# Second layer of tile 0 first and once for all kinds of steps, the third tile in a branch behind it, and evictions as one ScalarE operation

## The chip, the core and the metric

The program runs on one core of one Trainium2 chip. Times are device microseconds (us) of one launch, from the first to the last instruction of the core and the little that lies around it. The core has five engines with a queue each: TensorE (PE; its weight loads are listed apart as PEld), VectorE (DVE), ScalarE (ACT), GpSimd (POOL) and SyncE (SP). Each engine has a sequencer that reads its instructions, takes the branches and loads registers itself, and hands the rest to the engine; in the rows its instructions carry a q (PEldq, ACTq).

## The reference

Linear attention with positive random features on 8 batches of 8 heads, and then a mixture of 8 experts in which each of the 4608 tokens goes to one expert:

```python
    q_p, k_p = (phi(q_s), phi(k_s))
    kv = np.einsum('bhsm,bhsd->bhmd', k_p, v)
    ...
    return (num / den).astype(np.float32)
...
    expert_idx = np.argmax(logits, axis=1)
    ...
    for e in range(E):
        mask = expert_idx == e
        xe = x[mask]
        h = np.maximum(xe @ w1[e], 0.0)
        ye = h @ w2[e]
        out[mask] = gate_w[mask, None] * ye
```

x has 512 columns, the hidden layer 1024. The change lies in the experts alone, in `h @ w2[e]` and the scaling by the gate.

## The kernel before

The first part of the program (attention, and the routing that sorts tokens by expert) is written out without branches. Its result lies in DRAM as rows of tokens, which the second part gathers by index.

The second part runs in steps, one after the other, each for one expert. A step has two tiles of 128 tokens (256 columns in the first layer), and at the end of an expert perhaps a third one, full or of up to 64 tokens. So there are three kinds of steps, known only at run time: a register `kind` holds 2 for a step of two tiles, 1 for one with a half third tile ("short"), 0 for one with a full third tile. Every step is written out once, with all its variants, and branches on all engines pick one. `step` (L1134) issues, in this order: transposing loads for the next step; a split of new weights, where the expert changes; the first layer `l1`, in two parts with three variants each; gathers for a later step; `following()`, which prepares the input of the next step on ACT and DVE; and the second layer (L1149 to L1158).

Matrices are split into a high and a low part (`hh`, `hl`; `w2h`, `w2l`, both "w2p" in the rows), and three products are added. `l2(t, a)` (L1068) is the second layer of one tile: 24 matmuls of 512 columns, 3 for each of 8 chunks of the hidden layer. Its sum lies in a PSUM bank of its own: p_t for tile 0, p_snu for tile 1, p_skv for the third tile. `l2half` (L1081) does the short tile in 16 matmuls and needs a chain of ACT, DVE and ACT to evict. `send` (L1100) evicts a bank in halves, one by ACT (L1102) and one by DVE (L1103), both scaled by the gate, and `scatter` (L1106) writes the rows to the output by index on POOL, one scatter after the other.

The order on each engine is that of the code. Before, a step of kind 2 runs l2 of tile 0, loads a flag into a register (`reg`, L961) and runs l2 of tile 1 inside `when` (L1111). A step of another kind jumps behind that (L1149), runs the third tile (short or full, L1153) and then tiles 0 and 1 without asking. So the second layer of tiles 0 and 1 stands in the program twice.

What the code doesn't show is how an If is closed. Semaphores count the finished instructions of an engine, and all ways through an If must leave the same count. Where a way issues fewer instructions than another, the missing count is added to one of its own instructions; a way that issues nothing on an engine gets an instruction of the sequencer, which waits until the engine's own count stands where it should and then adds the rest. In the listings of the order it shows as a branch that "waits" for its own engine.

Of the kernel before, what the change touches and what calls it, by code (L numbers as in the profile page):

```python
# [14 lines left out]
AF = mybir.ActivationFunctionType  # L15
# [6 lines left out]
DM = H * D  # L22
# [824 lines left out]
class Experts:  # L847
# [121 lines left out]
    def split(self, n, cs=range(8)):  # L969
        for c in cs:  # L970
            split_r(self.nc, *self.part(n, c), self.nc.scalar, self.nc.vector)
# [126 lines left out]
        self.send(p, self.ys[i % 3], self.gt[i % 6], idx[:, i:i + 1])  # L1098

    def send(self, p, y, gate, idx):  # L1100
        c = DM // 2
        self.nc.scalar.activation(y[:, :c], p[:, :c], AF.Copy, scale=gate)  # L1102
        self.nc.vector.tensor_scalar_mul(y[:, c:], p[:, c:], gate)  # L1103
        self.scatter(y, idx)

    def scatter(self, y, idx):  # L1106
# [27 lines left out]
    def step(self, t, following, split=lambda: None):  # L1134
        engines = (ET.PE, ET.DVE, ET.Activation, ET.Pool)
        if t + 1 < NPR:
            self.flips(t + 1)
            self.flips3(t + 1)
        split()
        kind = self.kind(t, engines)  # L1140
        self.l1(t, kind)
        if t + 2 < NPR:
            self.gather(t + 2)
            self.gather3(t + 2)
        if t == 1:
            self.next(0, 2)
        following()
        self.nc.gpsimd.drain()
        with self.tc.If(kind > 1) as pair:  # L1149
            self.l2(t, 0)  # L1150
            self.when(self.reg(4, t, 1, engines), lambda: self.l2(t, 1))
        with pair.Else():
            with self.tc.If(kind > 0) as short:  # L1153
                self.l2half(t)
            with short.Else():
                self.l2(t, 2)
            for a in range(2):
                self.l2(t, a)  # L1158

    def tail(self, t):  # L1160
        split = lambda: self.change(t, 2)
# [103 lines left out]
```

## Time and profile before

| | us |
|---|---|
| median of 3 runs | 672.81 (671.24 to 673.86) |
| profiled execution, its own time | 671.42 |
| its span, first to last instruction | 669.4 |
| PE busy in the span | 639.6 (96%) |
| ACT, DVE, POOL busy | 409.7, 354.0, 280.1 |
| granted TensorE clock, mean | 0.997 |

The steps begin at about 270 us, the last matmul ends at 661.9 us. Busy time is that of engine instructions; register loads, branches and semaphore instructions aren't counted in it and are read line by line. Idle time is given with what ended it.

### The profile page before, as it was taken

To read this page: it belongs to the slowest core of one execution; us is meant where nothing else is said; L and a number is where in the kernel's file an instruction comes from. 1 tells how busy PE (TensorE), PEld (TensorE's weight loads), DVE (VectorE), ACT (ScalarE), POOL (GpSimd) and SP (SyncE) were. 2 spreads that over 40 slices of the span, in tenths; PEclk is the share of its full clock that TensorE was granted. 3 is DMA by queue.
4 is the path that set the end of the run, shared out by engine and by line. 5 is a ranking of instruction groups with operands and counts; after the bars stand their busy time and mean duration, and the time that the engine had idled before them with its cause. 6 is when DMAs were issued, how large, how long until landed. Compare 5 with 4: busy or idle time off the path is not lost. (4 is left out here: it accounts for less than half of the span.)

```text
span 669.4 us, 19369 instructions
## 1 busy us (share of the span) xinstructions
PE 639.6 (96%) x7185; PEld 579.0 (86%) x7185; DVE 354.0 (53%) x855; ACT 409.7 (61%) x1010; POOL 280.1 (42%) x499
## 2 busy tenths in 40 slices
PE   6898999999998989999999999999999999999995
PEld 5798999899898976788998989988989979989884
DVE  3467989989889978822222255222245255222220
ACT  6999999999999977633424166134256265243320
POOL 8576766676667932533330303312203303322111
PEclk9999999999999999999999999999999999999998
DMA  8864475655736342575641209543229509632101
GB/s 214 229 202 147 141 215 150 175 165 161 218 108 195 110 156 47 164 243 135 132 98 25 74 12 309 141 91 76 66 67 257 155 12 273 186 87 49 41 12 39
DMA packets 113247, 90.01 MB, mean 134 GB/s; under 512 B 72126, under 2 KB 96702, under 8 KB 113088
## 3 DMA queue, kind: packets, MB, share of 16 engines
q1 hardware_dynamic: 105360, 68.78, 38.6%
q0 software_dynamic: 7184, 19.04, 8.5%
q8 instruction: 92, 1.51, 0.9%
q14 instruction: 67, 0.55, 0.3%
q10 hardware_dynamic: 544, 0.13, 0.1%
HBM read 63.46 MB, written 19.15 MB: 123 GB/s over the span
## 5 line engine op out<-in xcount | busy, mean ns | idle before, releaser
L1032 PE MATMUL p<-xh,w1p 128*128 128x256 f32 (+2 forms) x960 | 148.0, 296 | 0.1
L1032 PEld LDWEIGHTS p<-xh,w1p 128*128 128x128 f32 x960 | 135.1, 188 | 2.5 <-issue 1.1
L1046 ACT ACTIVATE hh<-p 128x512 fp32r<-128x512 f32 (+2 forms) x84 | 43.6, 522 | 130.0 <-PE p L1032 126.1
L1047 DVE SCALAR_TENSOR_TENSOR hl<-p,hh 128x512 fp32r<-128x512 f32 (+2 forms) x84 | 48.1, 576 | 120.2 <-ACT hh L1046 117.3
L1107 POOL DMA_INDIRECT out_dram<-ys,idx x32 | 36.0, 1126 | 164.8 <-DVE ys L1103 57.6
L221 DVE TENSOR_REDUCE mx<-pp 128x8 f32<-128x1024 f32 x64 | 77.9, 1217 | 16.7 <-PE pp L214 16.3
L233 ACT ACTIVATE qp<-pp,mx 128x128 f32<-128x128 f32 x256 | 86.5, 585 | 0.0
L233 ACT ACTIVATE kp<-pp,mx 128x128 f32<-128x128 f32 x256 | 84.4, 547 | 2.7 <-DVE mx L221 2.0
L1032 PE MATMUL p<-xl,w1p 128*128 128x256 f32 (+2 forms) x480 | 83.3, 295 | 0.0
L214 PE MATMUL pp<-om_t,tq 64*128 64x128 f32 x1024 | 74.3, 284 | 3.9 <-ACT qp L233 3.0
L192 ACT COPY tq<-tt 128x1024 f32<-128x1024 f32 x59 | 73.3, 1243 | 0.9 <-PE tt L150 0.9
L1032 PEld LDWEIGHTS p<-xl,w1p 128*128 128x128 f32 x480 | 70.4, 188 | 0.0
L249 POOL TENSOR_TENSOR k<-kp 128x256 f32<-128x256 f32 x64 | 46.7, 730 | 52.6 <-ACT kp L233 49.0
L214 PEld LDWEIGHTS pp<-om_t,tq 64*128 64x128 f32 x1024 | 62.1, 187 | 7.5 <-ACT qp L233 4.5
L1006 ACT COPY xw<-xt 128x1024 uint16<-128x1024 uint16 x36 | 48.6, 1350 | 5.3 <-DMA xt<-xg 4.1
L1107 POOL DMA_INDIRECT out_dram<-y,idx x6 | 5.9, 986 | 105.6 <-DVE y L1103 56.5
L48 DVE TENSOR_TENSOR xl<-xw,xh 128x512 fp32r<-128x512 f32 x36 | 24.9, 693 | 46.6 <-ACT xh L54 36.8
L1102 ACT ACTIVATE ys<-p_snu,gt 128x256 f32<-128x256 f32 x16 | 7.6, 475 | 66.2 <-PE p_snu L1075 51.1
L1075 PE MATMUL p_t<-w2p,hl 128*128 128x512 f32 x120 | 47.0, 392 | 0.0
L1075 PE MATMUL p_snu<-w2p,hl 128*128 128x512 f32 x120 | 47.0, 391 | 0.0
L1073 PE MATMUL p_snu<-w2p,hh 128*128 128x512 f32 x120 | 47.0, 391 | 0.0
L1074 PE MATMUL p_t<-w2p,hh 128*128 128x512 f32 x120 | 47.0, 391 | 0.0
(407 smaller groups left out, 1337.3 us busy)
## 6 DMA issues: line engine op xcount, KB each, us to landing
w1s<-in_moe_w_dram SPq DMA_DIRECT2D x5, 2048.0 KB, 9.4
w2s<-in_moe_w_dram SPq DMA_DIRECT2D x5, 2048.0 KB, 10.5
v<-in_v_dram SPq DMA_DIRECT2D x32, 256.0 KB, 3.9
token_rows<-xc SPq DMA_DIRECT2D x8, 1024.0 KB, 4.8
k<-in_k_dram SPq DMA_DIRECT2D x31, 256.0 KB, 5.1
q<-in_q_dram SPq DMA_DIRECT2D x31, 256.0 KB, 5.5
kr<-in_k_dram SPq DMA_DIRECT2D x16, 64.0 KB, 3.6
vz<-in_v_dram SPq DMA_DIRECT2D x16, 64.0 KB, 3.9
```

Of the source, the lines that this page charges most:

```text
L192: self.nc.scalar.copy(self.pack(i, j), tt)
L214: nc.tensor.matmul(pp[:, a, n, i, :], th[r, k].rearrange("p a t -> p (a t)"), self.om[r, :], start=True, stop=True)
L221: nc.vector.tensor_reduce(out=mx[:, :, n], in_=s[("pp", h)][:, :, n], axis=AX.X, op=ALU.max, negate=True)
L233: nc.scalar.activation(x[:, j, :], pp[:, j % 2, n, j // 2, :], AF.Exp, bias=mx[:, j % 2, n, j // 2:j // 2 + 1])
L249: add = lambda o, x, y: nc.gpsimd.tensor_tensor(out=o, in0=x, in1=y, op=ALU.add)
L1006: self.nc.scalar.copy(x.bitcast(U16).rearrange("p c (t k) -> p k c t", k=2), xt.rearrange("p (k c) t -> p k c t", k=2))
L1032: self.nc.tensor.matmul(o, w[:, i, c], x[:, i, :], start=k == 0, stop=k == len(ops) - 1)
L1046: self.nc.scalar.activation(a[:, :, :n], o[:, :, :n], AF.Relu)
L1047: low = lambda d, c: self.nc.vector.scalar_tensor_tensor(out=d, in0=o[:, :, c], scalar=0.0, in1=a[:, :, c].bitcast(F32), op0=ALU.max, op1= ...
L1073: nc.tensor.matmul(p, h, self.w2h[:, c, :], start=c == 0, stop=False)
L1074: nc.tensor.matmul(p, h, self.w2l[:, c, :], start=False, stop=False)
L1075: nc.tensor.matmul(p, l, self.w2h[:, c, :], start=False, stop=c == self.NF - 1)
```

## The change

Every step now begins its second layer with tile 0, whatever its kind. Behind it stands an If without an Else for the third tile (`kind < 2`), and behind that tile 1, inside `when`, for all kinds. And `send` evicts a whole bank by one ACT instruction.

```diff
     def send(self, p, y, gate, idx):
-        c = DM // 2
-        self.nc.scalar.activation(y[:, :c], p[:, :c], AF.Copy, scale=gate)
-        self.nc.vector.tensor_scalar_mul(y[:, c:], p[:, c:], gate)
+        self.nc.scalar.activation(y, p, AF.Copy, scale=gate)
         self.scatter(y, idx)
...
-        with self.tc.If(kind > 1) as pair:
-            self.l2(t, 0)
-            self.when(self.reg(4, t, 1, engines), lambda: self.l2(t, 1))
-        with pair.Else():
+        self.l2(t, 0)
+        with self.tc.If(kind < 2):
             with self.tc.If(kind > 0) as short:
                 self.l2half(t)
             with short.Else():
                 self.l2(t, 2)
-            for a in range(2):
-                self.l2(t, a)
+        self.when(self.reg(4, t, 1, engines), lambda: self.l2(t, 1))
```

On PE, in the second layer of the first written-out step, this stood before between the matmuls of tile 0 (p_t) and tile 1 (p_snu) of a step of kind 2, and behind them (L1112 is `when`, L1153 the choice of the third tile; "ISA x2" are register operations):

```order
L1075 MATMUL p_t_5896<-w2p_5980,hl 128x512
L961 TENSOR_LOAD flags [waits DVE_49]
L961 ISA x2
L1112 COMPARE_AND_BRANCH
L1073 MATMUL p_snu<-w2p_5980,hh 128x512
...
L1112 UNCONDITIONAL_BRANCH
L1112 UNCONDITIONAL_BRANCH [waits PE_49]
L1153 COMPARE_AND_BRANCH
L1088 MATMUL p_skv<-w2p_5980,hh 128x512
```

The row that waits for PE itself is there the way on which tile 1 is left out. At the same place of PE this stands now (L1148 is the new If, L1149 the choice of the third tile, L1110 `when`):

```order
L1148 COMPARE_AND_BRANCH
L1149 COMPARE_AND_BRANCH
L1088 MATMUL p_skv<-w2p_5980,hh 128x512
...
L1149 UNCONDITIONAL_BRANCH
L1148 UNCONDITIONAL_BRANCH [waits PE_49]
L961 TENSOR_LOAD flags [waits DVE_49]
L961 ISA x2
L1110 COMPARE_AND_BRANCH
L1073 MATMUL p_snu<-w2p_5980,hh 128x512
```

The third tile has moved between the two tiles. The row that waits for PE itself is now the way of a step of kind 2, which has no third tile, and the register load and the branch stand behind it.

On ACT, in the same step, the difference of the evictions is this (ys and y are the rows to be scattered):

```order
-L1102 ACTIVATE ys_5989<-p_t_5896,gt 128x256
-L961 TENSOR_LOAD flags
-L1112 COMPARE_AND_BRANCH
-L1102 ACTIVATE ys_5987<-p_snu,gt 128x256
...
+L1101 ACTIVATE ys_5989<-p_t_5896,gt 128x512
+L1017 UNCONDITIONAL_BRANCH
+L1148 COMPARE_AND_BRANCH
+L1149 COMPARE_AND_BRANCH
+L1092 COPY y_5993<-p_skv 64x512
+L1094 ACTIVATE y_5993<-y_5993,gt 64x512
```

The evictions have twice the columns, tile 0's stands ahead of the third tile's, and the rows of DVE (L1103) are gone.

## Rows read from the trace of the kernel before

**Rows 1.** Busy time and granted clock by stretch (steps; the end).
```profile
core 0: us, PE busy (x) PEld busy (x) DVE busy (x) ACT busy (x) POOL busy (x), PEclk, DMA share, GB/s
335.00:663.00 328.00, 325.17 (x1873) 292.55 (x1871) 107.38 (x204) 131.28 (x211) 74.83 (x101) 1.00 0.39 105
663.00:669.40 6.40, 0.00 (x0) 0.00 (x0) 0.01 (x1) 0.00 (x0) 0.97 (x1) 0.67 0.14 51
```

**Rows 2.** Groups by line: busy us, mean ns | idle before, releaser.
```profile
L1075 PE MATMUL p_t<-w2p,hl 128*128 128x512 f32 x120 | 47.0, 392 | 0.0
L1075 PE MATMUL p_snu<-w2p,hl 128*128 128x512 f32 x120 | 47.0, 391 | 0.0
L1088 PE MATMUL p_skv<-w2p,hh 128*128 128x512 f32 x24 | 9.5, 396 | 1.6 <-DVE hh L1047 1.6
L1075 PE MATMUL p_skv<-w2p,hl 128*128 128x512 f32 x24 | 9.4, 393 | 0.0
```

**Rows 3.** Timeline of PE, 538 to 541: start, us, instruction [idle before].
```profile
538.03 0.75 PE L1032 MATMUL p<-xl,w1p 128*128 128x320 f32 x4
540.38 0.48 PE L1088 MATMUL p_skv<-w2p,hh 128*128 128x512 f32 x1 [1.60 <-DVE hh L1047]
```

**Rows 4.** Line 1149, then 1153, around 538: ns min/median/max, first to last start.
```profile
L1149 PEldq COMPARE_BRANCH  x1: 3141/3141/3141, 537.0 to 537.0; - x1
...
L1153 PEldq COMPARE_BRANCH  x1: 65/65/65, 540.1 to 540.1; - x1
```

**Rows 5.** Timeline of PE where tile 1 follows tile 0 (419).
```profile
419.25 0.39 PE L1075 MATMUL p_t<-w2p,hl 128*128 128x512 f32 x1
419.49 0.39 PE L1073 MATMUL p_snu<-w2p,hh 128*128 128x512 f32 x1
```

**Rows 6.** Line 1112 on PE's sequencer, 415 to 417.
```profile
L1112 PEldq COMPARE_BRANCH  x1: 65/65/65, 416.3 to 416.3; - x1
```

**Rows 7.** Timeline, the end: the last matmul, its eviction, the last scatter.
```profile
661.47 0.39 PE L1075 MATMUL p_snu<-w2p,hl 128*128 128x512 f32 x1
662.02 0.47 ACT L1102 ACTIVATE ys<-p_snu,gt 128x256 f32<-128x256 f32 x1 [5.15 <-PEq L1167]
662.53 0.48 DVE L1103 TENSOR_SCALAR ys<-p_snu,gt 128x256 f32<-128x256 f32 x1 [5.14 <-ACT ys L1102]
663.29 0.97 POOL L1107 DMA_INDIRECT out_dram<-ys,idx  x1 [4.62 <-POOLq L1149]
```

**Rows 8.** Line 1167 on PE's sequencer, 650 to 669.
```profile
L1167 PEldq COMPARE_BRANCH  x2: 181/1828/3474, 657.7 to 662.2; - x2
L1167 PEldq EVENT_SEMAPHORE  x2: 51/51/51, 661.9 to 662.0; - x2
```

**Rows 9.** Lines 1149, 961 and 1060 on PE's sequencer, 398.5 to 400.3.
```profile
L1149 PEldq EVENT_SEMAPHORE  x1: 51/51/51, 399.0 to 399.0; - x1
L961 PEldq TENSOR_LOAD <-flags x1: 307/307/307, 399.2 to 399.2; - x1
L961 PEldq FUSED_REGOPS  x1: 146/146/146, 399.6 to 399.6; - x1
L961 PEldq SEQ_ASSERT  x1: 18/18/18, 399.8 to 399.8; - x1
L1060 PEldq COMPARE_BRANCH  x1: 78/78/78, 399.9 to 399.9; - x1
```

**Rows 10.** Lines 961, 1060 and 1063 on PE's sequencer, all steps.
```profile
L961 PEldq TENSOR_LOAD <-flags x27: 297/308/656, 269.8 to 629.1; - x27
L1060 PEldq COMPARE_BRANCH  x48: 70/222/1893, 270.7 to 637.9; - x48
L1063 PEldq COMPARE_BRANCH  x18: 65/216/2711, 337.8 to 644.8; - x18
```

**Rows 11.** ACT instructions by line (1102, 930, 1094).
```profile
L1102 ACT ACTIVATE ys<-p_snu,gt x16: 474/475/477, 268.1 to 662.0; 128x256 f32<-128x256 f32 x16
L930 ACT ACTIVATE h<-p x4: 574/586/602, 257.2 to 258.7; 128x512 f32<-128x512 f32 x4
L1094 ACT ACTIVATE y<-y,gt x3: 724/724/724, 400.2 to 652.3; 64x512 f32<-64x512 f32 x3
```

## The prediction

> **What bounds the kernel now.** I read first the busy time by stretch [rows 1]: from 335 to 663 us, twelve of the steps, PE is busy for 325.17 of 328.00 us at the full granted clock, ACT for 131, DVE for 107, POOL for 75. The reader is to see that 2.83 us are left idle in all, so PE alone sets the time, an engine beside it costs nothing while PE isn't waiting for it, and anything that stops PE's queue is paid in full. Then where these 2.83 us lie. In the groups by line only one row of the second layer has idle time before it, the short third tile with 1.6 us [rows 2]; the timeline shows it once, at 540.38 [rows 3]. The rest is the end: the last matmul runs from 661.47 for 0.39 [rows 7], so it ends at 661.86, 1.14 us before 663.00. Third, the instructions of PE's sequencer, which aren't in busy time [rows 4, 6, 8 to 10].
>
> The counts of the groups also give the kinds of steps. p_t has 120 low products, 8 a step: 15 steps. p_skv has 24 of L1088, 8 a step: 3 short steps; and 24 of L1075: 3 with a full third tile [rows 2]. That leaves 15 - 3 - 3 = 9 steps of kind 2. All 15 have a tile 1 (p_snu x120).
>
> **The change part by part.** No matmul is added or removed. What changes is what stands between them.
>
> *The stall at 538 goes.* The profile puts it down to DVE, but that is the wait that came last in time; the branch row tells more. At 537.0 the jump over the two-tile variant took PE's sequencer 3.141 us, till 540.14, and only then the short tile's branch (540.1) and its first matmul (540.38) follow [rows 3, 4]. The last first-layer matmul began at about 538.5, so the jump began 1.5 us of queued work ahead and was not covered. In the changed program tile 0 follows the first layer without this jump, and the jumps of a third tile begin behind tile 0, whose matmuls are longer, 0.23 apart [rows 5]. At the one place where a branch among them can be timed, `when` at 416.3, the first matmul behind it began at 419.49: 3.2 us ahead [rows 5, 6]. That covers a jump of 3.141. Gain: the 1.60 idle and 0.09, by which the first matmul behind it is longer (0.48 against 0.39) [rows 3, 5]: 1.7 us. If the cover fails the gain is zero.
>
> *A wait is added in the nine steps of kind 2.* They have no third tile, so on the way round the new If PE's sequencer waits for PE's own count, behind the last matmul of tile 0, and adds the rest. Before, such a step only loaded a register there, 3.2 us ahead of need. Queued behind the wait are the register load, its operations, the branch, and all of tile 1. Does such a wait hold until the matmul has finished? The kernel before does it on PE once, at its end: the jump of 3.474 from 657.7 ends at 661.2, yet the semaphore instruction of the same line stands at 661.9, just behind the end of the last matmul at 661.86 [rows 7, 8]. It held the sequencer for 0.7 us, until nothing was left in PE. The Trainium skill (PSUM — Partial Sum Buffer, Engine vs sequencer instructions) says that the sequencer waits only for earlier instructions to be dispatched and not for their end; by that rule alone the bare addition would cost nothing and the sum would be rival A's. The row at 661.9 shows that the instruction here has a wait of its own.
>
> The price of one, from one matmul's start to the next, against the usual 0.23:
> - the last matmul of tile 0 runs 0.39 [rows 5]: 0.16 more;
> - from its end to the semaphore instruction, 661.86 to 661.9 [rows 7, 8]: 0.04;
> - semaphore instruction, register load, register operations, assertion, branch: the same five in the same order at the end of a step of another kind, from 399.0 to 399.9 + 0.08 [rows 9]: 0.95 (starts are given to a tenth);
> - from a branch's end to the first matmul of an empty PE, 540.1 + 0.065 to 540.38, with a semaphore instruction between [rows 3, 4]: 0.2, of which I take 0.12;
> - that first matmul, slower by 0.09 as above.
>
> 0.16 + 0.04 + 0.95 + 0.12 + 0.09 = 1.36 us, nine times: 12.2 us. Nothing covers it, since PE is what everything else waits for. From below: a wait alone, with the load somehow out of the way, would be 0.16 + 0.04 + 0.12 + 0.09 = 0.4, or 3.7 us in all; less than nothing is excluded, as the sequencer reaches the place 3.2 us early. From above: the slowest register load was 0.656, 0.35 over its median [rows 10], and the way round the If is itself a taken jump, of which the slowest on a similar place took 2.711 [rows 10], and the slowest of all 3.474 [rows 8]; 0.3 of that would be beyond a cover of 3.2: 2.0 each, 18 us. I take 1.36, since every piece is a row of its own, and the median load.
>
> *Steps of kinds 0 and 1.* They pass no such wait: both ways of the inner If have matmuls of their own to carry the count. The register load that they newly do (0.3 to 0.66 [rows 10]) lies 3 us ahead of need. Tile 0 needs the last chunk of the hidden layer only with its eighth chunk, 21 matmuls of 0.23 = 4.8 us in. Price zero; if PE did wait there, the only such wait of before, 1.6 [rows 3], is the bound.
>
> *Evictions.* Each goes from 0.475 on ACT and then 0.48 on DVE [rows 7, 11] to one ACT operation of 512 columns. No row shows one with a gate from PSUM: the nearest are 0.586 (512 columns from PSUM, no gate) and 0.724 (512 columns with the gate, from SBUF) [rows 11]; I take 0.70, nearer to that with the gate. Off the end it hides under PE: ACT is idle for more than half of the stretch, and no matmul waits for these banks until the next step's second layer, some 10 us on. At the end it is on the path: ACT 662.02, DVE until 663.01, scatter at 663.29 [rows 7]. Now the scatter may start at 662.02 + 0.70 + 0.28 = 663.00: 0.29 earlier; between 0.17 and 0.41 by the two rows. The last step has a short third tile, whose ACT, DVE, ACT chain now lies under tile 1's 24 matmuls (5.5 us). Should its scatter be late, the last one waits, and the 0.3 is lost.
>
> *Sum.* On the profiled execution's own time of 671.42 (span 669.4): + 12.2 - 1.7 - 0.3 = + 10.2, so 681.6. The median of the three runs, 672.81, lies 1.4 above it; I don't know which the new runs will be nearer to and add half: 682.3.
>
> **Rivals.**
> A, *the wait costs nothing* (the way round the If holds no wait in the chip's program, or PE has enough queued to bridge it). For it: PE has bridged nearly all branches until now. Against: a wait for one's own last matmul can't be bridged by one's own queue, and the row at 661.9. Then only the gains stay: 671.42 - 2.0 = 669.4, or 670.8 against the median. It is the way to "not slower", and decides once one wait costs less than 2.0 / 9 = 0.22 us.
> B, *the jump itself stalls*. The new If moves nine steps across a jump in the middle of the second layer. Jumps of PE mostly took 0.07 to 0.22, and a few took 1.893, 2.711, 3.141 and 3.474 [rows 4, 8, 10], at some places of the program and not at others. If all nine were slow ones, at 3.474 against a cover of 3.2, 0.3 each is added to the drain: 9 x 0.3 = 2.7, 685.0; if the cover were only the 1.5 of the place at 537.0, 2.0 each, 18, 700. Against: of 48 jumps of L1060 the median is 0.22 [rows 10]. The Trainium skill (Runtime: NRT & Kernel Launch, Instruction fetch mechanics) says that a taken branch whose target isn't in the fetched window must wait for a transfer of instructions; by it some of the nine would be slow and most not. The trace agrees, with one long jump among several short ones on each line.
> C, *the gains don't come*: the stall at 538 turns up at another jump of the third tile, and the last scatter waits. For it: the program is shorter, so all targets shift. Then 682.3 + 2.0 = 684.3.
>
> **How the numbers follow.** Forecast 0.72, A 0.07, B 0.09, C 0.09, and 0.03 for gains that I don't see. 0.5%, some 3.4 us, is about what a measurement of this kernel can tell from no change. Forecast, B and C are slower, A is within; half of the last 0.03 is faster: faster 0.02, same 0.08, slower 0.90. The forecast's own range is one wait between 1.0 and 1.7, 9.0 to 15.3, that is 678.5 to 686. To hold 8 in 10 it is stretched to 677.5 and, to take in most of B, to 687.5; A and the far end of B stay outside.
>
> **What would show it.** Right: in each of nine steps a gap of about 1.6 us between the start of the last p_t and of the first p_snu matmul, ended by the sequencer; PE's idle time from 335 to the end higher by 1.1 to 1.3 for each such step there; L1148's semaphore instruction on PE nine times; no gap there in the six other steps; no idle time before L1088; ACT's evictions at about 0.70 and DVE's gone; the scatter about 1 us, not 1.4, behind the last matmul's end. Wrong: p_snu following p_t after 0.23 in steps of kind 2 (then A), or gaps over 2.2 there, with long L1148 branches ahead (then B). The granted clock must stay at 1.00 around the gaps, as it did from 335 to 663 with a gap of 1.6 in it [rows 1, 3]; if it falls, all numbers here are too low.

## The result, and the profile after

The changed kernel is slower: 680.72 us median of 6 runs (679.49 to 682.83) against 671.44 (670.74 to 673.86) of the kernel before, ratio 1.013 with an interval of 1.0107 to 1.0152. The forecast was 682.3, its range 677.5 to 687.5. The profiled execution took 680.55 with a span of 678.8.

Where the 9.4 us between the spans lie is read from the idle time of PE. This is the view of waits of the kernel after, PE, from 262 us on (line waited for: us in total, times, longest):

```profile
PE p_snu L1073 <- PEq L1148: 6.1, 6, 1.0
PE p_snu L1073 <- issue: 4.0, 3, 1.4
PE p L1032 <- issue: 0.5, 1, 0.5
```

Nine waits stand before the first matmul of tile 1, as many as there are steps of kind 2: 10.1 us of idle time. Six are put down to PE's own sequencer at the new If and three to "issue", which means that nothing was waited for that the profile shows; these are the same wait: at all nine places the semaphore instruction of the new If stands 0.04 us behind the end of tile 0's last matmul, and the register load and the branch follow it. The one wait of before, ahead of L1088 [rows 2, 3], is gone, and a short one of 0.5 has come up inside the first layer. The groups by line say the same (busy us, mean ns | idle before, releaser):

```profile
L1073 PE MATMUL p_snu<-w2p,hh 128*128 128x512 f32 x120 | 47.8, 399 | 10.0 <-PEq L1148 6.1 <-issue 4.0
L1088 PE MATMUL p_skv<-w2p,hh 128*128 128x512 f32 x24 | 9.4, 393 | 0.0
```

One of the nine places at close range, the timeline of PE at 423 us (start, us, instruction [idle before]):

```profile
423.37 0.40 PE L1075 MATMUL p_t<-w2p,hl 128*128 128x512 f32 x1
425.05 0.49 PE L1073 MATMUL p_snu<-w2p,hh 128*128 128x512 f32 x1 [1.28 <-issue]
```

Where before 0.24 us passed from one start to the next [rows 5], 1.68 pass. The shortest of the nine gaps is 1.400 and the longest 1.818; they add up to 13.61. What PE's sequencer does in one of the short gaps, at 338 us, where tile 0's last matmul ends at 338.08 and tile 1's first begins at 339.09 (lines 1148, 961 and 1110 of the kernel after, from 336 to 340; ns min/median/max, first to last start):

```profile
L1148 PEldq EVENT_SEMAPHORE  x1: 51/51/51, 338.1 to 338.1; - x1
...
L961 PEldq TENSOR_LOAD <-flags x1: 307/307/307, 338.3 to 338.3; - x1
L961 PEldq FUSED_REGOPS  x1: 146/146/146, 338.7 to 338.7; - x1
L961 PEldq SEQ_ASSERT  x1: 18/18/18, 338.9 to 338.9; - x1
...
L1110 PEldq COMPARE_BRANCH  x1: 67/67/67, 339.0 to 339.0; - x1
```

These are the five instructions of [rows 9] in the same order. The first of them comes only behind the end of tile 0's last matmul (338.08), and the first matmul of tile 1 only behind the last of them.

The stretch of the steps and the end (columns as in [rows 1]):

```profile
335.00:672.30 337.30, 329.22 (x1886) 294.45 (x1884) 94.87 (x177) 139.13 (x213) 77.01 (x101) 1.00 0.38 101
672.30:678.80 6.50, 0.06 (x1) 0.00 (x0) 0.00 (x0) 0.69 (x1) 0.99 (x1) 0.72 0.14 49
```

The matmul work is what it was, and the granted clock is 1.00. PE is idle for 8.08 us of the 337.30, where it was 2.83 of 328.00 with the 1.14 of the end in it [rows 1]. Two of the nine gaps lie ahead of this stretch.

The timeline of the end, PE, ACT and POOL:

```profile
671.97 0.39 PE L1075 MATMUL p_snu<-w2p,hl 128*128 128x512 f32 x1
672.54 0.69 ACT L1101 ACTIVATE ys<-p_snu,gt 128x512 f32<-128x512 f32 x1 [3.55 <-PEq L1162]
673.50 0.99 POOL L1105 DMA_INDIRECT out_dram<-ys,idx  x1 [3.31 <-ACT ys L1101]
```

The last scatter starts 1.14 us behind the end of the last matmul (672.36), where it was 1.43 [rows 7]. DVE has no part in it any more.

The steps begin at the same time in both executions (first matmul of the first step at 274.4), and the last matmul ends 10.5 later. Added up from start to start of neighbouring matmuls: within the second layer + 12.3, from the first layer to the second - 1.8, from the second to the next first layer - 0.1, within the first layer 0.0 (the new wait of 0.5 is balanced by shorter ones), in all + 10.5. The end is 1.1 shorter: 9.4.

### The profile page after: what moved, and what is told of

It reads as the page before. It is cut to its first block, busy times and chain, and to the rows that moved or that the text cites. A ratio compares the mean times of both kernels' runs of the same rounds, so it can differ in the third digit from the quotient of the medians.

```text
span 678.8 us, 19349 instructions
## 1 busy us (share of the span) xinstructions
PE 641.2 (94%) x7185; PEld 578.2 (85%) x7185; DVE 337.6 (50%) x820; ACT 416.9 (61%) x1010; POOL 282.5 (42%) x499
## 3 DMA queue, kind: packets, MB, share of 16 engines
q8 instruction: 86, 1.41, 0.9%
## 5 line engine op out<-in xcount | busy, mean ns | idle before, releaser
L1101 ACT ACTIVATE ys<-p_snu,gt 128x512 f32<-128x512 f32 x16 | 11.0, 689 | 76.8 <-PE p_snu L1075 68.5
L1074 PE MATMUL p_t<-w2p,hh 128*128 128x512 f32 x120 | 46.9, 391 | 0.0
L1073 PE MATMUL p_t<-w2p,hh 128*128 128x512 f32 x120 | 46.9, 391 | 0.0
```

The lines of the kernel that those rows point to most:

```text
L1073: nc.tensor.matmul(p, h, self.w2h[:, c, :], start=c == 0, stop=False)
L1074: nc.tensor.matmul(p, h, self.w2l[:, c, :], start=False, stop=False)
```

## The experiments

The theory: the loss is a drain. In each step of kind 2 PE's sequencer waits at the empty way of the new If until PE has finished, and only then reads the flag and branches. Rivals: the jump past the third tile stalls; the eviction by one instruction is what costs; or the new order does.

**The flag is loaded before the first layer.** The wait stays, and the register load moves out from behind it. This is the kernel after with this edit:

```diff
         kind = self.kind(t, engines)
+        one = self.reg(4, t, 1, engines)
         self.l1(t, kind)
...
-        self.when(self.reg(4, t, 1, engines), lambda: self.l2(t, 1))
+        self.when(one, lambda: self.l2(t, 1))
```

> The changed kernel, with the flag of tile 1 loaded into its register ahead of the first layer; wait, jump and evictions stay. Theory (the wait for PE's own last matmul stops the sequencer, and all that is queued behind it is paid): the register load and its operations, about 0.7 of the 1.36 us, leave each of the nine gaps; 680.7 - 6.3 = 674.4 us, gaps of about 0.9 from start to start. Rival jump (a slow taken jump round the If is what costs): no change, 680.7. Rival eviction (the longer ACT evictions hold something up): no change, 680.7.

Measured: 673.65 us (672.29 to 678.42), ratio to before 1.0022 (0.9995 to 1.0048). The timeline of PE at 336 us:

```profile
335.31 0.40 PE L1075 MATMUL p_t<-w2p,hl 128*128 128x512 f32 x1
336.02 0.49 PE L1073 MATMUL p_snu<-w2p,hh 128*128 128x512 f32 x1 [0.32 <-PEq L1149]
```

and its semaphore instructions at the new If (here L1149) on PE's sequencer, all and the one at this place:

```profile
L1149 PEldq EVENT_SEMAPHORE  x9: 51/51/51, 290.8 to 595.9; - x9
...
L1149 PEldq EVENT_SEMAPHORE  x1: 51/51/51, 335.7 to 335.7; - x1
```

The matmul ends at 335.71 and the semaphore instruction stands at 335.7. All nine gaps are there, each of 0.70 to 0.71 instead of 1.40 to 1.82 (0.9 had been expected). So the wait lasts until the matmul has finished. By itself, with the branch behind it, it costs 0.48 over the usual 0.23, and 0.1 for the slower first matmul; the rest of the price was the register load with its operations. That makes 7.2 us less by the gaps (13.61 - 6.41) and 7.3 by the ratios to before (1.0130 - 1.0022, of 673). The jump is not in it: of those at L1149 the four slow ones took 1.11, 2.77, 3.26 and 3.38 us here, and the gaps behind them are no longer than the others.

**The empty way gets a matmul of its own.** Then the count is carried by an instruction that nobody has to wait for. The added matmul writes 128 columns into a bank that is not read in such a step:

```diff
-        with self.tc.If(kind < 2):
+        with self.tc.If(kind < 2) as more:
...
+        with more.Else():
+            self.nc.tensor.matmul(self.p_2[2][:, :P], self.chunk(self.hh, t, 0)[:, 0, :P], self.w2h[:, 0, :P],
+                                  start=True, stop=True)
         self.when(self.reg(4, t, 1, engines), lambda: self.l2(t, 1))
```

> The changed kernel, with an Else at the If of the third tile that issues one matmul of 128 columns into the unused bank of the third tile, so that the count is carried by it and no wait is needed; jump, load and evictions stay. Theory: the gaps go and nine matmuls of 0.15 to 0.2 come: 680.7 - 12.4 + 1.6 = 669.9 us. Rival jump: still 680.7 and the 1.6, 682. Rival eviction: 680.7 and the 1.6, 682.

Measured: 673.00 (670.85 to 677.68), ratio 1.0005 (0.9982 to 1.0028). The drain is gone: in six of the nine steps the three intervals from tile 0's last matmul over the added one to tile 1's second add up to 0.58, 0.12 more than two usual ones. But the time is 3 us above the 669.9 that I expected. Some 1.5 of that may lie in the runs that it is compared with, since before had a median of 672.92 there and 671.44 in the runs of the result. And the profile shows three stalls that I had not counted, two at the jump and one in the first layer. The timeline of PE at 521 us (the first at the jump) and at 536 us (the one in the first layer):

```profile
521.13 0.40 PE L1075 MATMUL p_t<-w2p,hl 128*128 128x512 f32 x1
521.54 0.33 PE L1154 MATMUL p_skv<-w2p,hh 128*128 128x128 f32 x1
522.38 0.49 PE L1073 MATMUL p_snu<-w2p,hh 128*128 128x512 f32 x1 [0.51 <-issue]
...
537.44 0.41 PE L1032 MATMUL p<-xh,w1p 128*128 128x320 f32 x1 [1.25 <-issue]
```

and the jump of L1148 on PE's sequencer, before the stall at 521 and before the other one at the jump, at 575:

```profile
L1148 PEldq COMPARE_BRANCH  x1: 4014/4014/4014, 517.5 to 517.5; - x1
...
L1148 PEldq COMPARE_BRANCH  x1: 3935/3935/3935, 570.6 to 570.6; - x1
```

The jump ends at 521.5, when tile 0's matmuls are just used up, and the register load behind it comes too late. Each of these two costs about 1.0, the one at 536 about 1.4, some 3 us in this execution. So rival B was real, a slow jump, but it is not the nine gaps: this kernel keeps the jump, and the gaps are gone.

**Tile 1 inside both ways.** Neither way is empty on PE, and the register load lies as far ahead of need as before:

```diff
         self.l2(t, 0)
-        with self.tc.If(kind < 2):
+        with self.tc.If(kind > 1) as pair:
+            self.when(self.reg(4, t, 1, engines), lambda: self.l2(t, 1))
+        with pair.Else():
...
-        self.when(self.reg(4, t, 1, engines), lambda: self.l2(t, 1))
+            self.l2(t, 1)
```

> The changed kernel, with an If and an Else behind tile 0: steps of kind 2 go straight to tile 1, the others do the third tile and then tile 1, which stands in both ways. No way is empty on PE, and no wait for its own count is left. Theory: the changed kernel without its nine waits, 680.7 - 12.4 = 668.3 us, which is below the kernel before by the stall at 538 and the end. Rival jump: the same, since the jump in the middle of nine steps goes as well. Rival eviction: 680.7.

Measured: 668.72 (666.50 to 671.88), ratio 0.9939 (0.9915 to 0.9964), faster than both kernels. The row by stretch of the steps, and the branch of the If on PE's sequencer:

```profile
335.00:661.40 326.40, 326.31 (x1882) 294.31 (x1880) 94.20 (x176) 138.26 (x212) 75.41 (x101) 1.00 0.39 105
```

```profile
L1148 PEldq COMPARE_BRANCH  x15: 65/65/217, 289.4 to 647.8; - x15
L1148 PEldq EVENT_SEMAPHORE  x6: 51/51/51, 372.2 to 657.0; - x6
```

PE is idle for 0.09 us in 326.40. The six semaphore instructions are those of the steps with a third tile. Order and evictions are those of the kernel after. The empty way is gone, and with it some 12 us. The jump round the third tile in the middle of the nine steps is gone as well, so this run alone doesn't tell the wait from the jump; the version with the added matmul, which keeps the jump, does.

**The kernel after with the evictions of before**, in halves by ACT and DVE:

```diff
-        self.nc.scalar.activation(y, p, AF.Copy, scale=gate)
+        c = DM // 2
+        self.nc.scalar.activation(y[:, :c], p[:, :c], AF.Copy, scale=gate)
+        self.nc.vector.tensor_scalar_mul(y[:, c:], p[:, c:], gate)
```

> The changed kernel with the old evictions, half by ACT and half by DVE. Theory: all of the loss stays, and the end is longer by 0.3: 681.0 us. Rival eviction: most of the 9.3 us come back, 672. Rival jump: 681.0.

Measured: 680.68 (679.40 to 683.34), ratio 1.0117 (1.0088 to 1.0145): no different from the kernel after. The evictions are not the loss. One of its nine gaps is longer, on the timeline of PE at 579 us and by its jump of L1150 (the new If here):

```profile
579.15 0.39 PE L1075 MATMUL p_t<-w2p,hl 128*128 128x512 f32 x1
581.78 0.49 PE L1073 MATMUL p_snu<-w2p,hh 128*128 128x512 f32 x1 [2.24 <-PEq L1150]
```

```profile
L1150 PEldq COMPARE_BRANCH  x1: 5242/5242/5242, 575.5 to 575.5; - x1
```

The jump ends at 580.7, 1.2 behind tile 0's last matmul (579.5); the gap is 2.63 instead of 1.40. That is rival B in one step of nine.

**A wait put into the kernel before.** Behind tile 0, in the way of kind 2, stands an If that is never taken (the If around it has made sure that `kind` is 2), so that it adds an empty way and nothing else:

```diff
         with self.tc.If(kind > 1) as pair:
             self.l2(t, 0)
+            with self.tc.If(kind < 2):
+                self.nc.tensor.matmul(self.p_2[2][:, :P], self.chunk(self.hh, t, 0)[:, 0, :P], self.w2h[:, 0, :P],
+                                      start=True, stop=True)
             self.when(self.reg(4, t, 1, engines), lambda: self.l2(t, 1))
```

> The kernel before, with an If for kind < 2 put behind tile 0 inside the way of kind 2. It is never taken, so its matmul never runs; all it does in the nine steps is that PE's sequencer waits for its own count. Order and evictions are those of before. Theory (the wait is the whole loss): nine gaps of 1.4 to 1.8 us from start to start come, at 1.3 each of cost, 11.5 to 12.5 us over the kernel before, about 684. Rival (the loss comes with the new order or the evictions, and such a wait is bridged): as before, 672.

Measured: 683.47 (681.75 to 687.15) against 673.09, ratio 1.0164 (1.0134 to 1.0194). The timeline of PE at 425 us:

```profile
425.03 0.40 PE L1075 MATMUL p_t<-w2p,hl 128*128 128x512 f32 x1
426.44 0.49 PE L1073 MATMUL p_snu<-w2p,hh 128*128 128x512 f32 x1 [1.01 <-DVEq L1112]
```

Nine gaps again, 1.405 to 1.643. The profile names DVE's sequencer here, but this is the same gap with the same length at the same place; the named engine only came last in time. This If jumps over no third tile, the order is that of before, and the evictions are too. The wait, with the load and the branch that are queued behind it, makes the loss without the rest of the change. The stall at L1088 isn't there in this kernel, though its order is that of before; one of 1.30 stands in the first layer at 543 instead, during a jump of L1060 of 2.95.

**The new order alone**, in the kernel before, for the steps with a third tile:

```diff
         with pair.Else():
+            self.l2(t, 0)
             with self.tc.If(kind > 0) as short:
...
-            for a in range(2):
-                self.l2(t, a)
+            self.l2(t, 1)
```

> The kernel before, with its If and Else as they were, but in the Else tile 0 first, then the third tile, then tile 1; evictions as before. The jump at the end of the first layer stays ahead of tile 0. Theory on the stall at 538 (the jump is slow there): it stays, PE stops for 1.5 to 2 us before a matmul of tile 0 in a short step, and the time is that of before within 0.3%. Rival (DVE's last operation is what was waited for, as the profile names it): tile 0 needs it only 4.8 us later, so the stall goes and the time is 1.7 us (0.25%) below before. The trace tells better than the time.

Measured: 672.55 (669.85 to 674.51), ratio 0.9988 (0.9970 to 1.0006). My expectation missed: I expected that the jump of L1149 would stay slow and the stall at 538 with it. Instead the jump took at most 0.35, and PE stalled elsewhere. The branch over all steps on PE's sequencer, and the timeline of DVE and PE at 567 us:

```profile
L1149 PEldq COMPARE_BRANCH  x15: 73/73/350, 285.8 to 649.7; - x15
```

```profile
566.33 0.69 DVE L1047 SCALAR_TENSOR_TENSOR hl<-p,hh 128x512 fp32r<-128x512 f32 x1 [2.60 <-ACT hh L1046]
...
567.33 0.39 PE L1075 MATMUL p_t<-w2p,hl 128*128 128x512 f32 x1
570.88 0.39 PE L1073 MATMUL p_t<-w2p,hh 128*128 128x512 f32 x1 [3.16 <-issue]
```

These are the third and the fourth chunk of one tile. No branch stands between them, and the last product of ACT and DVE for this tile had been ready since 567.0 (566.33 + 0.69). The run can't tell whether the stall of before was the jump's, since the jump and the stall went together. The trace of the kernel before can. This is the same matmul in another of its short steps, with DVE's last product of that step:

```profile
388.47 0.40 PE L1088 MATMUL p_skv<-w2p,hh 128*128 128x512 f32 x1
...
389.48 0.21 DVE L1047 SCALAR_TENSOR_TENSOR hh<-p,hh 128x64 fp32r<-128x64 f32 x1
```

The matmul starts 1.2 us before that product ends (389.69), and in the third short step it does too (646.93 and 648.16). So at 540 it was not DVE's last product that PE had to wait for, though the profile names it. The jump at L1149 took 0.225 us in this step, and 3.141 before the stall.

**The eviction alone**, in the kernel before (L1102 and L1103 become one ACT instruction, as in the diff of the change):

```diff
-        c = DM // 2
-        self.nc.scalar.activation(y[:, :c], p[:, :c], AF.Copy, scale=gate)
-        self.nc.vector.tensor_scalar_mul(y[:, c:], p[:, c:], gate)
+        self.nc.scalar.activation(y, p, AF.Copy, scale=gate)
```

> The kernel before, with the one ACT eviction alone. Theory: only the end gets shorter, by 0.3 us for the earlier scatter, so the time is that of before within what can be measured (0.9975 to 1.001 of it); the stall at 538 stays. Rival (ACT gets longer and holds up the first layer): slower by up to 0.2 x 30 = 6 us.

Measured: 672.93 (669.89 to 675.83), ratio 0.9993 (0.9967 to 1.0019): no difference that can be measured. The stall at 540 and a slow jump before it (L1147 here, the L1149 of before) are there as before. The timeline of PE and the row of the branch:

```profile
541.76 0.47 PE L1088 MATMUL p_skv<-w2p,hh 128*128 128x512 f32 x1 [1.43 <-DVE hh L1047]
```

```profile
L1147 PEldq COMPARE_BRANCH  x15: 73/73/2974, 286.7 to 646.6; - x15
```

## Why the prediction was right, point by point

**The nine waits: right in mechanism and size.** 13.61 us of gaps less 9 x 0.23 is 11.5, and nine first matmuls of 0.49 instead of 0.39 make 0.9: 12.4 against 12.2. Piece by piece: 0.16 for the last matmul, as taken; from its end to tile 1's first matmul 1.01 in the short gaps, where 0.04 + 0.95 + 0.12 = 1.11 had been taken; 0.1 for the slow first matmul, as taken. Six gaps are 1.40 to 1.42, so they cost 1.27 where 1.36 had been taken. Three are longer, by 0.25 to 0.41: two by a slow register load (0.56 instead of 0.31 at 447.8, 0.63 at 314.8), and at 423 the assertion comes 0.27 later behind the register operations, for which no row gives a reason. So the pieces were 0.8 us too large over the nine places, and the median load left out 0.9 us at three of them. That the two errors cancel, so that 12.2 meets 12.4, is luck. The bound from below, a wait with the load out of the way, was 0.4; the early load measured 0.48 + 0.1. That the wait suffices was shown by the If added to the kernel before, that its removal brings the time back by the two kernels without an empty way.

**The stall at 538 goes: right in this execution, its reason borne out, its going in part luck.** The way from the first layer to the second is 1.77 shorter in the sum over all steps, 1.7 predicted. The reason given (the jump of L1149 is slow and not covered) fits the traces: a slow jump and the stall stand together before and with the eviction alone, and the other short steps of before exclude the wait for DVE. But with the new order alone, and with the wait added to the order of before, neither turned up at this place, and in both PE stalled elsewhere. So the change of order was not needed to lose this stall, nor does it keep a stall away: in the kernel after PE waits 0.5 within the first layer at 543. What makes a jump slow in one program and not in another stayed open; the last section has what the traces show of it.

**The end: - 1.1 instead of - 0.3.** The eviction took 0.688 where 0.70 was taken, and the scatter moved by the 0.29 predicted; with the eviction alone it starts 1.14 us behind the last matmul as well, and with the old evictions in the kernel after 1.43. From the scatter's start to the end of the span 5.3 us pass instead of 6.1; these 0.8 I had not seen, and they stay open. The eviction is not enough for them: with it alone 6.1 pass, and with the old evictions in the kernel after 5.6. By the eviction alone the median does not move by anything that can be told.

**Rival A** fell with the first profile. **Rival B** was half right: of the nine jumps at L1148 three were slow, as this row and their times of 1.12, 3.92 and 3.98 us show (line 1148 of the kernel after, PE's sequencer):

```profile
L1148 PEldq COMPARE_BRANCH  x15: 71/231/3975, 287.3 to 658.9; - x15
L1148 PEldq EVENT_SEMAPHORE  x9: 51/51/51, 291.4 to 603.6; - x9
```

They cost nothing here, since the two long ones began 4.0 us ahead of the end of tile 0 (523.5 with 527.51, and 576.0 with 580.04) and not 3.2: the gaps behind them are of 1.40, among the shortest. So the prediction put the cover too low at 3.2, and the slowest jump too low at 3.474. That both errors cancel is luck: the jumps ended 0.14 and 0.07 us before tile 0 did. In the kernel with the old evictions one of 5.24 didn't fit, and cost its 1.2. The prediction also read one long jump to a line from the maxima of [rows 10]; in the trace of before L1060 has three of 0.9 us and more among its 48, and L1063 two among its 18. **Rival C** came true for a part: a stall in the first layer instead of that at L1088, shorter by 1.1. No scatter was late.

**The sum.** + 12.4 - 1.8 - 1.1, and - 0.1 that I hadn't, is + 9.4 on the span; predicted + 10.2. The difference is the end's 0.8. The 0.7 that the forecast added for the median of before was not needed: that median was 671.44 in the runs of the result.

The profile of the version with tile 1 in both ways is 1.6 us shorter than that of before, its median 4.2. The larger number is the one to trust, with its interval of 2.4 to 5.7. Most of the difference lies ahead of the steps: in that execution the granted clock was 0.50 for 3.4 us from 24.85 on, and the first matmul of the steps came at 276.53 instead of 274.35. From there to the end of the span it is 3.9 us shorter (391.2 for 395.1).

## What to carry to other kernels

An If without an Else wasn't free on the way round it. Where its body has work on an engine, the sequencer waited on the empty way until that engine had finished, and everything behind the wait (a register load, a branch) was paid on an empty engine: 1.27 to 1.7 us each time here, 0.58 without the load. Give the other way work of its own on the bounding engine, by moving into both ways something that has to be done anyway, as the version of 668.72 does; and put register loads ahead of such a place. When a change moves code, leave 1 to 3 us of the forecast's range to stalls of PE: beside the nine waits, seven of the nine programs had some of 0.4 to 3.2 us, mostly at different matmuls, and two had none. Each program has one profile, so how far they also differ from one execution to the next is not shown; the two executions with the longest stalls, 674.51 with the new order alone and 683.34 with the old evictions, were the slowest of their kernels.

## What was not expected of the hardware

A slow jump on PE's sequencer lasts from 0.9 to 5.2 us in the nine traces. What it costs depends on how many matmuls PE still has queued when it begins. In the second layer, behind tile 0, the slow jumps began 4.0 to 4.1 us before these were used up, and only the one of 5.24 (old evictions) and those of 3.94 and 4.01 (added matmul) cost 0.9 us or more. At the end of the first layer the queued matmuls lasted 1.8 us (536.95 to 538.78 before), and a jump of 3.14 cost 1.60 us of idle time.

PE can also stand still without a jump and with all its inputs there, as for the 3.16 us of the kernel with the new order alone, in a stretch in which the DMA engines were full. The traces show what it has in common with the slow jumps. The DMA queue q8, of the kind "instruction", brings 16 KB at a time; this is its row in the DMA view of that stall (567.72 to 570.88):

```profile
q8 instruction: 1, 0.02, 1.9%
```

By its packet in the trace the transfer lasts from 568.50 to 569.47, and PE goes on 1.41 us behind its end. All 46 jumps of 0.9 us and more in the steps of the nine traces end 1.3 to 1.5 us behind the end of such a transfer, that of 538 too (538.69 and 540.09). There are five stalls of some 0.4 us and more that stand at neither a slow jump nor one of the nine waits, among them those at 543 in the kernel after and at 536 with the added matmul; they end 1.25 to 1.43 behind one. Of all moments in the steps only some 6 in 100 lie 1.2 to 1.65 us behind one. So the traces point to late instructions in both cases. No run changes how they are loaded, so this cause is not shown by experiment.

Behind the stall of 3.16 TensorE ran at its lower level. The rows by stretch of that kernel:

```profile
560.00:567.50 7.50, 7.10 (x53) 6.58 (x53) 3.15 (x5) 2.57 (x4) 4.18 (x5) 1.00 0.79 213
567.50:571.20 3.70, 0.54 (x3) 0.30 (x3) 1.42 (x2) 2.51 (x4) 1.73 (x4) 1.00 1.03 393
571.60:575.00 3.40, 3.40 (x10) 2.63 (x9) 0.00 (x0) 0.00 (x0) 0.00 (x0) 0.51 0.59 156
575.00:580.00 5.00, 5.00 (x23) 4.11 (x22) 0.48 (x1) 0.47 (x1) 1.03 (x1) 0.99 0.87 101
```

For 3.4 us, from 0.8 us behind the stall on, the granted clock is 0.51, that is 1.2 GHz, and 10 matmuls run where, at 0.23 each, some 15 would. The same happened behind the gap of 2.63 (2.24 idle) with the old evictions:

```profile
579.30:581.80 2.50, 0.26 (x3) 0.03 (x1) 0.48 (x1) 0.47 (x1) 0.53 (x3) 1.00 0.83 293
582.50:586.50 4.00, 4.00 (x12) 3.16 (x12) 0.00 (x0) 0.00 (x0) 1.03 (x1) 0.59 0.70 135
```

It did not happen behind the gaps of 1.40 to 1.82 of the kernel after, in the stretch of which the clock is 1.00. So the two stalls of 3.16 and 2.24 us idle cost 1 us or more on top of their length. In the steps of the nine traces the clock fell behind these two alone, and the longest other stall was 1.60 idle [rows 3].
